# Banks for attention tiles ahead of the down groups, the first down groups in two parts at the turn of the halves, and one table load left out, in a kernel that mixes attention and a SwiGLU FFN

## Chip, cores, metric

The kernel runs on 1 core of one Trainium2 chip. The metric is the device time of one execution in microseconds (us); runs are given as median and range. The profile is that of one execution, with its own time.

## What is computed

`x` is 2048 x 576. The output mixes two branches by a gate per row:

```python
x = A_x
g = _sigmoid((x * gate_w).sum(-1, keepdims=True))
a = _A_ref(x, A_wq, A_wk, A_wv, A_wo, A_beta)   # 32 heads of 18, 4 segments of 512
b = _B_ref(x, B_w_gate, B_w_up, B_w_down)       # (silu(x @ w_gate) * (x @ w_up)) @ w_down
return g * a + (1 - g) * b
```

In `_A_ref` each segment has causal softmax attention within itself, `p @ v` of `softmax(q k^T)`, mixed by a gate per head with what a memory of the earlier segments returns; the heads' outputs, side by side, go through `wo`. The FFN's inner width is 4608.

## The kernel before

**Stages.** Up to about 220 us the kernel projects `q`, `k`, `v` and works the memory. Then one loop over `seq` (72 steps) does the FFN and, woven into it, the softmax attention. A last stage sends attention's output through `wo` and mixes. The FFN runs over two halves of 1024 rows; each half goes over 36 f-tiles of 128 of the inner width. fp32 operands are split into a high and a low part, and each product is made of three (`split`, L127: ScalarE copies the high part, L128; VectorE subtracts for the low part, L129; `split_by`, L939, does the same a beat apart, L940 and L941).

**One f-tile.** Seven products `seven(t, j)` (L993) build the gate and up projections of the tile from sums of blocks. Each is six matmuls of 512 columns at L998 and one at L1001. They accumulate in PSUM banks 0 (`a`), 1 (`x`) and 2 (`y`); ScalarE copies between them (L1058 among them) and VectorE adds. Two Silu (L1075, L1077) need their function's table on ScalarE, and `exp_table()` (L990) right behind them runs a dummy Exp of one column so that the Exp table is loaded again before attention's next Exp; so each f-tile shows two table loads, listed at L1075 and L991. The product of the two projections is `hh` (high) and `hl` (low). In the third tile of three its first half is split by L128 and L129 as one deferred step.

**The beats.** Between the products stand eight calls of `tick`, numbered 0 to 7, and each calls `beat(k, half)` (L943). A beat does, in this order: the steps deferred to it (`due`: loads, splits, weight sums), down groups in the number that `SHARE = (0, 0, 2, 2, 3, 3, 3, 3)` allows, and a step of the attention generator whenever its credit (`TICK`) reaches 1.

**Down groups.** After every third f-tile sixteen down groups are listed in `groups` (L1012), eight row blocks by two column parts of 320 and 256, each over the three f-tiles just made. A group is nine matmuls at L851, `hh`, `hh`, `hl` for each of three f-tiles; VectorE then copies it into `ya` (L854, the first time) or adds it (L856). They are worked in ticks 2 to 7 of the next f-tile, which is the first of the next three. At the turn of the halves, after f-tile 35 of the first half, there is no next tile in this half, and the sixteen groups are worked in ten beats of their own (`BREAK`, L1094), in which `x_second` (L966) also loads, sums and splits the second half's operands.

**Attention.** A step does several of: scores of a tile (`s_bank`, matmul L720 into a bank from `ts_tile`, row maxima by VectorE at L726), Exp of the previous tile (`e_bank`, ScalarE L738), high and low part of its result (VectorE L752, GpSimd L753), a transpose by DMA, and every sixth step the values (`v_unit`, matmuls L768 and L769 into one more bank from `ts_tile`, read by VectorE at L775).

**Banks.** Banks 0, 1 and 2 belong to `seven`. Group tiles take the one of banks 3, 4 and 7 that was taken longest ago. Score and value tiles take the one taken longest ago out of 5 and 6 while any group is listed, and out of 5, 6, 7, 3, 4 when none is. A matmul into a bank waits until the bank's former readers are done: the Exp (L738) of a score tile, L775 of a value tile, L854 or L856 of a group.

**The end.** When the attention generator has run out, `c_open` (L864) opens the last stage: it defers six loads of parts of `wo` and, by `c_load`, loads of attention's output `o` and the memory's part `me` of the first two row tiles. `c_tr` adds `me` to `o` on GpSimd (L913, L914) and transposes on TensorE (L917, L919); products with `wo` follow at L151. All DMAs are issued by the queue on SyncE (SP).

Of the kernel before, what the change touches and what calls it, by code (L numbers as in the profile page):

```python
# [12 lines left out]
F32 = mybir.dt.float32  # L13
# [7 lines left out]
P = 128  # L21
S = 2048
D = 576
# [4 lines left out]
FT = 36  # L28
# [7 lines left out]
CH = 3  # L36
# [5 lines left out]
HALF = ((2, 3), (0, 1))  # L42
TICK = ((0.57, 1.0), (0.47, 1.0))
QUIET = (5, 6, 7)
LEAD = 3
HIGH = (2, 3, 3, 7, 7, 8, 9)
LOW = (5, 6, 7, 8, 9, 10, 11)
# [18 lines left out]
def gated_mix(ctx, tc, xT, xrest, wf, wfr, wfh, wd, wv, wo, beta, cmask, ident, bmask, out):  # L66
    nc = tc.nc
# [18 lines left out]
    ps = pool(ctx, "ps", 1, space=bass.MemoryType.PSUM)  # L86
# [18 lines left out]
    pair_tile = banks(3, 4)  # L105
# [4 lines left out]
    x_tile = banks(1)  # L110
    y_tile = banks(2)
    taken = {}

    def oldest(*ids):
        n = min(ids, key=lambda i: taken.get(i, 0))
        taken[n] = len(taken) + max(taken.values(), default=0) + 1
        return n

    def ts_tile(shape=(P, L)):
        return ps.tile(list(shape), F32, name=f"bank{oldest(5, 6) if groups else oldest(5, 6, 7, 3, 4)}")  # L120

    def group_tile(shape=(P, L)):
        return ps.tile(list(shape), F32, name=f"bank{oldest(3, 4, 7)}")

    groups = []

# [153 lines left out]
    with ExitStack() as st:  # L280
# [310 lines left out]
        for s in range(NSEG):  # L591
# [41 lines left out]
            if s == 3:  # L633
# [50 lines left out]
    with ExitStack() as st:  # L684
# [3 lines left out]
        def defer(k, fn):  # L688
            while len(due) < k:
                due.append([])  # L690
            due[k - 1].append(fn)
# [146 lines left out]
            nc.sync.dma_start(f32(d).rearrange("p a n -> p (a n)"), dc[f])  # L838
            return d

        def down_group(c, i, hf, hs, ws, ya, half):
            b, k = divmod(i, 4)
            cs = (slice(0, 320), slice(320, D))[hf]
            t = (pair_tile if cps else group_tile)([P, 320])[:, :cs.stop - cs.start]
            n = 0
            for f in range(CH * c, CH * c + CH):
                hh, hl = (z[:, b, P * k:P * k + P] for z in hs[half, f])
                d = ws[half, f]
                dh, dl = d[:, 0], d[:, 1]
                for p, q in ((hh, dh), (hh, dl), (hl, dh)):  # L850
                    nc.tensor.matmul(t, p, q[:, cs], start=(n == 0), stop=(n == 3 * CH - 1))  # L851
                    n += 1
            if c == 0:
                nc.vector.tensor_copy(ya[:, i, cs], t)  # L854
            else:
                nc.vector.tensor_add(ya[:, i, cs], t, ya[:, i, cs])  # L856
            if c == FT // CH - 1 and hf and half == 0:
                stores.append((ffd[i], ya[:, i]))
# [5 lines left out]
        def c_open():  # L864
            if cps:
                return
            ast.close()
            cps.append(pool(st, "cp", 2, side="right"))
            for hf in range(2):
                wos.append(cps[0].tile([P, 2, NT, 288], F32R, name=f"wo{hf}", bufs=1))  # L870
            for n, (hf, z) in zip((1, 2, 4, 5, 8, 9), ((0, 0), (0, 1), (0, 2), (1, 0), (1, 1), (1, 2))):
                wo_load(n, hf, slice(96 * z, 96 * z + 96))
            defer(2, lambda: tiles.update({0: c_load(0)}))
            defer(3, lambda: nc.scalar.activation(gg, gg, AF.Exp, scale=-1.0))
            defer(4, gates)
            defer(6, lambda: tiles.update({1: c_load(1)}))

        def gates():
            nc.vector.tensor_scalar_add(gg, gg, 1.0)
# [63 lines left out]
        def beat(k=None, half=0):  # L943
            for fn in due.popleft() if due else ():
                fn()
            busy = 1 if groups else 0
            share = 2 if k is None else SHARE[k]
            for n in range(max(share, 1)):
                if groups and n < share:
                    down_group(*groups.pop(0))  # L950
                if n % 2 or (not busy and (n or k in QUIET)):
                    continue
                credit[0] += 0.5 if k is None else TICK[half][busy]
                if credit[0] >= 1:
                    credit[0] -= 1
                    if next(att, att) is att:
                        c_open()
# [32 lines left out]
        def exp_table():  # L990
            nc.scalar.activation(bg[:, 0:1], idt[:, 0:1], AF.Exp)  # L991
# [15 lines left out]
        for pos, (half, f) in enumerate(seq):  # L1007
# [67 lines left out]
            nc.scalar.activation(sg0, sg0, AF.Silu)  # L1075
# [120 lines left out]
```

## Time and profile before

| what | us |
|---|---|
| median of 3 runs | 1739.13 |
| range of the runs | 1737.43 to 1739.77 |
| the profiled execution, its own time | 1738.29 |
| its span in the trace | 1736.6 |
| TensorE busy | 1714.6 |
| VectorE busy | 1370.0 |
| ScalarE busy | 1094.1 |
| GpSimd busy | 935.1 |

The profiled execution lies 0.84 us under the median. Its time is 1.7 us longer than its span, which runs from the first to the last instruction. In a row of the timeline the first number is the start in us from the span's start, the second the length; then engine, line, operation, output and inputs with bank numbers left out, shape, and how many alike follow one another; in square brackets how long the engine was idle just before and what ended that. PE is TensorE, PEld its weight loads, DVE VectorE, ACT ScalarE, POOL GpSimd. Matmuls overlap: the next one starts before the last one's end, so ends lie later than the next start.

### The profile page before, as it was taken

How to read it: one execution, taken by the hardware profiler on the slowest of the kernel's cores; microseconds unless marked ns; L12 is line 12 of the kernel's file. 1: busy time of each engine (PE TensorE's matmuls, PEld its weight loads, DVE VectorE, ACT ScalarE, POOL GpSimd, SP SyncE). 2: the span in 40 equal slices, each digit the busy share in tenths (PEclk: the TensorE clock that was granted, in tenths of full speed). 3: DMA queues.
4: the chain of work that ended last, by engine and by line, in shares of the span. 5: the costliest groups of instructions: out<-in, count | busy, mean ns of one | idle time of the engine just before them, and what ended most of it. 6: DMA issues, size and time to landing. Idle time of an engine off the chain costs nothing.

```text
span 1736.6 us, 34910 instructions
## 1 busy us (share of the span) xinstructions
PE 1714.6 (99%) x11868; PEld 1482.5 (85%) x11868; DVE 1370.0 (79%) x3231; ACT 1094.1 (63%) x2198; POOL 935.1 (54%) x1194
## 2 busy tenths in 40 slices
PE   9999999999999999999999999999999999999999
PEld 7899978888888888887887788888888888888899
DVE  6557588988899889887989677787888777887655
ACT  7766585776677567666755755665766576566511
POOL 4434645666666656565666455555555555555121
PEclk9999999999999999999999999999999999999999
DMA  8654499999998889997879976776778677766544
GB/s 281 237 185 155 149 306 191 222 215 203 202 232 197 176 205 207 190 190 193 205 149 266 265 173 142 180 178 162 152 180 182 139 155 180 169 135 166 157 148 137
DMA packets 524002, 328.05 MB, mean 189 GB/s; under 512 B 411184, under 2 KB 460336, under 8 KB 523824
## 3 DMA queue, kind: packets, MB, share of 16 engines
q1 hardware_dynamic: 523824, 325.83, 76.6%
q8 instruction: 93, 1.52, 0.4%
q14 instruction: 85, 0.70, 0.1%
HBM read 165.76 MB, written 76.09 MB: 139 GB/s over the span
## 4 chain that ended last, share of the span: by engine, by line
PE 81%; ACT 9%; DVE 4%; DMA 2%; issue 2%; POOL 1%; SPq 1%; DVEq 0%; ACTq 0%; POOLq 0%
PE bank L998 30%; PE bank L851 26%; PE bank L151 10%; PE bank L1001 5%; PE bank L720 4%; PE bank L768 2%; ACT L1075 1%; PE bank L769 1%; ACT L991 1%; ACT pe L738 1%; PE bank L406 1%; PE bank L452 1%; ACT row L1075 1%; PE bank L342 1%; DVE hl L941 1%
## 5 line engine op out<-in xcount | busy, mean ns | idle before, releaser
L753 POOL TENSOR_TENSOR p<-pe,p 128x512 f16<-128x512 f32 x320 | 374.9, 1171 | 454.1 <-DVE p L752 437.4
L851 PE MATMUL bank<-dw,hh 128*128 128x320 f32 (+1 forms) x2304 | 489.9, 305 | 2.7 <-ACT hh L128 1.4
L851 PEld LDWEIGHTS bank<-dw,hh 128*128 128x128 f32 x2304 | 382.6, 190 | 14.0 <-DVE ya L856 1.6
L738 ACT ACTIVATE pe<-bank,mb 128x512 f32<-128x512 f32 (+3 forms) x512 | 246.4, 523 | 218.8 <-DVE mb L726 213.4
L851 PE MATMUL bank<-dw,hl 128*128 128x320 f32 (+1 forms) x1152 | 341.1, 296 | 0.2 <-DVE hl L129 0.2
L726 DVE CUSTOM_DVE_ANT_0 scr<-bank,cm 128x512 bf16<-128x512 f32 (+3 forms) x512 | 246.3, 481 | 7.9 <-PE bank L720 1.2
L851 PEld LDWEIGHTS bank<-dw,hl 128*128 128x128 f32 x1152 | 218.6, 190 | 0.4 <-DVE hl L129 0.4
L856 DVE TENSOR_TENSOR ya<-bank,ya 128x320 f32<-128x320 f32 x352 | 157.7, 453 | 72.3 <-PE bank L851 71.6
L1001 PE MATMUL bank<-xr,rh 128*128 128x512 f32 x504 | 196.5, 390 | 0.0
L746 POOL TENSOR_SCALAR_AFFINE_SELECT pe<-pe 128x256 f32<-128x256 f32 (+1 forms) x320 | 151.1, 473 | 31.3 <-ACT pe L738 20.2
L752 DVE CAST p<-pe 128x512 f16<-128x512 f32 x320 | 147.5, 461 | 0.0
L256 POOL TENSOR_TENSOR ws<-raw 128x256 f32<-128x256 f32 x140 | 123.6, 883 | 18.3 <-DMA raw<-in_wf_dram 7.2
L720 PE MATMUL bank<-kst,qst 108*128 108x512 bf16 (+3 forms) x512 | 125.4, 306 | 4.7 <-ACT pe L738 4.7
L1001 PEld LDWEIGHTS bank<-xr,rh 128*128 128x128 f32 x504 | 94.7, 188 | 20.5
L941 DVE TENSOR_TENSOR hl<-row,hh 128x512 fp32r<-128x512 f32 x120 | 101.6, 847 | 10.9 <-ACT hh L940 10.6
L1068 ACT ACTIVATE row<-bank 128x512 f32<-128x512 f32 x72 | 43.1, 599 | 94.6 <-PE bank L1001 94.5
L1075 ACT ACT_TABLE_LOAD x72 | 92.4, 1283 | 1.3
L1073 DVE TENSOR_TENSOR row<-bank,row 128x512 f32<-128x512 f32 x72 | 49.7, 690 | 55.0 <-ACT bank L1072 54.9
L991 ACT ACT_TABLE_LOAD x72 | 92.4, 1283 | 1.0
L151 PE MATMUL bank<-xo,qhi 128*128 128x512 f32 x264 | 83.1, 396 | 0.1
L1072 ACT ACTIVATE bank<-bank 128x512 f32<-128x512 f32 x72 | 42.0, 584 | 65.0 <-PE bank L1001 64.6
L256 POOL TENSOR_TENSOR ws<-raw,ws 128x256 f32<-128x256 f32 x70 | 56.6, 808 | 48.4 <-DVE wo__22573 L263 10.9
(2166 smaller groups left out, 4119.1 us busy)
## 6 DMA issues: line engine op xcount, KB each, us to landing
raw<-in_wf_dram SPq DMA_DIRECT2D x140, 256.0 KB
rh<-rc SPq DMA_DIRECT2D x72, 336.0 KB
dc<-dw SPq DMA_DIRECT2D x36, 576.0 KB
dw<-dc SPq DMA_DIRECT2D x36, 576.0 KB
stk<-q SPq DMA_DIRECT2D x32, 384.0 KB
draw<-in_wd_dram SPq DMA_DIRECT2D x36, 288.0 KB
rc<-rt SPq DMA_DIRECT2D x42, 224.0 KB
vd<-vps SPq DMA_DIRECT2D x8, 912.0 KB
```

The lines of the kernel that those rows point to most:

```text
L151: nc.tensor.matmul(t, st[n], mv[n], start=(n == 0), stop=(n == 13))
L256: (nc.gpsimd.tensor_sub if sub else nc.gpsimd.tensor_add)(src[j], p(), q())
L720: nc.tensor.matmul(t[:, c:c + w], qs[:KR, pr, P * i:P * i + P], ks[:KR, pr, 0:w], start=True, stop=True)
L726: nc.vector.tensor_tensor_reduce(scr[:, :w], t[:, c:c + w], cm[:, L - w:L], -SCALE, 3.0e38, OP.add, OP.min, m[:, k:k + 1])
L738: nc.scalar.activation(pe[:, c:c + w], t[:, c:c + w], AF.Exp, bias=m[:, k:k + 1], scale=SCALE)
L746: nc.gpsimd.affine_select(d, d, pattern=pat, compare_op=OP.is_ge, fill=0.0, base=0, channel_multiplier=1)
L752: nc.vector.tensor_copy(p[:, 0], pe)
L753: nc.gpsimd.tensor_sub(p[:, 1], pe, p[:, 0])
L851: nc.tensor.matmul(t, p, q[:, cs], start=(n == 0), stop=(n == 3 * CH - 1))
L856: nc.vector.tensor_add(ya[:, i, cs], t, ya[:, i, cs])
L998: nc.tensor.matmul(t, w[:, p, z], x[z][:, q], start=first and n == 0, stop=False, skip_group_check=True)
L1001: nc.tensor.matmul(t, rem[:, RPOS[j]], XR[j], start=False, stop=True, skip_group_check=True)
```

## The change

It has four parts. (1) `ts_tile` also gives bank 7 to score and value tiles while sixteen groups are listed, none popped yet, and the groups aren't the last of a half; banks 5, 6, 7, 3, 4 when none is listed, 5 and 6 else. What is "oldest" is told by a clock that goes on by one with each beat and each tile, on which a score or value tile counts as taken four later (`HELD`) and a group's tile one later. (2) At the turn the first three groups are popped after the first of the ten beats and computed by `down_parts`: for all three first the f-tiles 33 and 34, then f-tile 35. (3) `exp_table()` is left out in f-tile 35 of both halves. (4) `c_open` defers the first two `c_load` ahead of the loads of `wo`, the second at 3 beats in place of 6. The core of the diff:

```diff
+HELD = 4
...
+    clock = [0]
+
+    def soonest(ids, held):
         n = min(ids, key=lambda i: taken.get(i, 0))
-        taken[n] = len(taken) + max(taken.values(), default=0) + 1
+        clock[0] += 1
+        taken[n] = clock[0] + held
         return n
 
     def ts_tile(shape=(P, L)):
-        return ps.tile(list(shape), F32, name=f"bank{oldest(5, 6) if groups else oldest(5, 6, 7, 3, 4)}")
+        ids = (5, 6, 7, 3, 4) if not groups else (5, 6, 7) if groups[0][0] < FT // CH - 1 and len(groups) == 16 else (5, 6)
+        return ps.tile(list(shape), F32, name=f"bank{soonest(ids, HELD)}")
 
     def group_tile(shape=(P, L)):
-        return ps.tile(list(shape), F32, name=f"bank{oldest(3, 4, 7)}")
+        return ps.tile(list(shape), F32, name=f"bank{soonest((3, 4, 7), 1)}")
...
+        def down_group(*z):
+            down_parts([z], CH)
+
+        def down_parts(some, *cuts):
+            ts = []
+            for a, e in zip((0,) + cuts, cuts):
+                for m, (c, i, hf, hs, ws, ya, half) in enumerate(some):
...
+                    for f in range(CH * c + a, CH * c + e):
...
+                    if e == CH:
+                        down_end(ts[m], *some[m])
...
+            defer(2, lambda: tiles.update({0: c_load(0)}))
+            defer(3, lambda: tiles.update({1: c_load(1)}))
             for n, (hf, z) in zip((1, 2, 4, 5, 8, 9), ((0, 0), (0, 1), (0, 2), (1, 0), (1, 1), (1, 2))):
                 wo_load(n, hf, slice(96 * z, 96 * z + 96))
-            defer(2, lambda: tiles.update({0: c_load(0)}))
             defer(3, lambda: nc.scalar.activation(gg, gg, AF.Exp, scale=-1.0))
             defer(4, gates)
-            defer(6, lambda: tiles.update({1: c_load(1)}))
...
             busy = 1 if groups else 0
+            clock[0] += 1
...
-            exp_table()
+            if f < FT - 1:
+                exp_table()
...
                     for n in range(BREAK):
                         beat(None if n > 1 else n)
+                        if n == 0:
+                            down_parts([groups.pop(0) for _ in range(3)], CH - 1, CH)
```

Rows of the two programs follow at three places. The first is on TensorE in ticks 1 to 4 of an f-tile that is the first of three (L1001 is L1018 in the change, L720 L724, L998 L1015, L851 L862). Before:

```order
L1001 MATMUL bank2_8520<-xr1_1579,rh1_2332 128x512
L720 MATMUL bank5_8609<-kst1_2324,qst1_2323 128x512
L998 MATMUL bank0_8519<-xo20_2273,wo__8452 128x512 x3
...
L851 MATMUL bank3_8636<-dw_8240,hh_7662 128x320 x2
...
L720 MATMUL bank6_8656<-kst1_2324,qst1_2323 128x512
L851 MATMUL bank4_8662<-dw_8240,hh_7662 128x256 x2
...
L851 MATMUL bank7_8691<-dw_8240,hh_7662 128x320 x2
```

The same place in the change:

```order
L1018 MATMUL bank2_8520<-xr1_1579,rh1_2332 128x512
L724 MATMUL bank7_8609<-kst1_2324,qst1_2323 128x512
L1015 MATMUL bank0_8519<-xo20_2273,wo__8452 128x512 x3
...
L862 MATMUL bank3_8636<-dw_8240,hh_7662 128x320 x2
...
L724 MATMUL bank5_8656<-kst1_2324,qst1_2323 128x512
L862 MATMUL bank4_8662<-dw_8240,hh_7662 128x256 x2
...
L862 MATMUL bank3_8691<-dw_8240,hh_7662 128x320 x2
```

No row has moved; the first score tile is on bank 7 instead of 5, the next on 5 instead of 6, and the third group on bank 3, which the first group has just had, instead of 7.

The second place is TensorE at the turn, behind the last score tile of the first half (`bank6`) and around the value unit (L768 and L769, in the change L772 and L773); `dw_12713`, `dw_12852` and `dw_12969` are the down weights of f-tiles 33, 34 and 35. Before:

```order
L720 MATMUL bank6_13036<-kst1_2324,qst1_2323 128x256
L768 MATMUL bank5_13058<-v_11896,pt_12703 128x57
...
L769 MATMUL bank5_13058<-v_11896,pt_12945 128x38
L851 MATMUL bank3_13115<-dw_12713,hh_12131 128x320 x2
...
L851 MATMUL bank3_13115<-dw_12852,hh_12669 128x320 x2
L851 MATMUL bank3_13115<-dw_12852,hl_12670 128x320
L851 MATMUL bank3_13115<-dw_12969,hh_12861 128x320 x2
```

In the change:

```order
L724 MATMUL bank6_13035<-kst1_2324,qst1_2323 128x256
L862 MATMUL bank7_13044<-dw_12713,hh_12131 128x320 x2
...
L862 MATMUL bank3_13051<-dw_12713,hh_12131 128x256 x2
...
L862 MATMUL bank4_13058<-dw_12713,hh_12131 128x320 x2
...
L862 MATMUL bank4_13058<-dw_12852,hl_12670 128x320
L862 MATMUL bank7_13044<-dw_12969,hh_12861 128x320 x2
L862 MATMUL bank7_13044<-dw_12969,hl_12862 128x320
L862 MATMUL bank3_13051<-dw_12969,hh_12861 128x256 x2
...
L772 MATMUL bank5_13090<-v_11896,pt_12703 128x57
```

Three groups have moved ahead of the value unit, their products with f-tiles 33 and 34 first and those with f-tile 35, which need the newest `hh` and `hl`, last; the value unit's bank 5 is now one whose former score tile is read by the Exp at the turn (third place).

The third place is ScalarE at the turn; `row_12867` holds the Silu of the gate, `hh_12861` is the last tile's high part, and `pe` is attention's Exp. Before:

```order
L1075 ACT_TABLE_LOAD
L1075 ACTIVATE row_12867<-row_12867 128x512
L1077 ACTIVATE row_12868<-bank2_12920 128x512
L991 ACT_TABLE_LOAD
L991 ACTIVATE bg_82<-idt_79 128x1
L128 ACTIVATE hh_12861<-row_12867 128x512
L738 ACTIVATE pe_13032<-bank7_12987,mb1_2326 128x128
```

In the change:

```order
L1092 ACT_TABLE_LOAD
L1092 ACTIVATE row_12867<-row_12867 128x512
L1094 ACTIVATE row_12868<-bank2_12920 128x512
L132 ACTIVATE hh_12861<-row_12867 128x512
L742 ACT_TABLE_LOAD
L742 ACTIVATE pe_13031<-bank5_12987,mb1_2326 128x128
```

The load of the Exp table has moved behind the copy of `hh`, to the first Exp that needs it, and the dummy Exp is gone. In the last f-tile of the second half, where no Exp of attention follows, ScalarE has three rows less.

More of the change, by code (lines that the diff above doesn't have):

```diff
@@ L112, in gated_mix @@
     taken = {}
-    def oldest(*ids):
+    clock = [0]
+    def soonest(ids, held):
         n = min(ids, key=lambda i: taken.get(i, 0))
-        taken[n] = len(taken) + max(taken.values(), default=0) + 1
+        clock[0] += 1
+        taken[n] = clock[0] + held
         return n
     def ts_tile(shape=(P, L)):
-        return ps.tile(list(shape), F32, name=f"bank{oldest(5, 6) if groups else oldest(5, 6, 7, 3, 4)}")
+        ids = (5, 6, 7, 3, 4) if not groups else (5, 6, 7) if groups[0][0] < FT // CH - 1 and len(groups) == 16 else (5, 6)
+        return ps.tile(list(shape), F32, name=f"bank{soonest(ids, HELD)}")
     def group_tile(shape=(P, L)):
-        return ps.tile(list(shape), F32, name=f"bank{oldest(3, 4, 7)}")
+        return ps.tile(list(shape), F32, name=f"bank{soonest((3, 4, 7), 1)}")
     groups = []
@@ L839, in d_fetch, with down_end @@
             return d
-        def down_group(c, i, hf, hs, ws, ya, half):
-            b, k = divmod(i, 4)
-            cs = (slice(0, 320), slice(320, D))[hf]
[L844 to L852, printed above, removed]
+        def down_group(*z):
[4 more added lines that the diff above has]
+                for m, (c, i, hf, hs, ws, ya, half) in enumerate(some):
+                    b, k = divmod(i, 4)
+                    cs = (slice(0, 320), slice(320, D))[hf]
+                    if a == 0:
+                        ts.append((pair_tile if cps else group_tile)([P, 320])[:, :cs.stop - cs.start])
+                    n = 3 * a
+                    for f in range(CH * c + a, CH * c + e):
+                        hh, hl = (z[:, b, P * k:P * k + P] for z in hs[half, f])
+                        d = ws[half, f]
+                        dh, dl = d[:, 0], d[:, 1]
+                        for p, q in ((hh, dh), (hh, dl), (hl, dh)):
+                            nc.tensor.matmul(ts[m], p, q[:, cs], start=(n == 0), stop=(n == 3 * CH - 1))
+                            n += 1
+                    if e == CH:
+                        down_end(ts[m], *some[m])
+        def down_end(t, c, i, hf, hs, ws, ya, half):
+            cs = (slice(0, 320), slice(320, D))[hf]
             if c == 0:
```

## Prediction

> **What bounds the kernel now.** The first view is the profile page, its totals of busy time and its chain of work that ended last:
>
> ```profile
> span 1736.6 us, 34910 instructions
> PE 1714.6 (99%) x11868; PEld 1482.5 (85%) x11868; DVE 1370.0 (79%) x3231; ACT 1094.1 (63%) x2198; POOL 935.1 (54%) x1194
> ...
> PE 81%; ACT 9%; DVE 4%; DMA 2%; issue 2%; POOL 1%; SPq 1%; DVEq 0%; ACTq 0%; POOLq 0%
> ```
>
> TensorE (PE) sets the time, and its matmuls stay the same in number and shape. So the change can win only where PE stands still or runs at a low clock, 22 us of idle time and a little more. The second view, PE's waits (total, times, longest, in us), says where; its two largest rows:
>
> ```profile
> PE bank L720 <- ACT pe L738: 4.7, 6, 1.2
> PE bank L768 <- ACT pe L738: 3.1, 2, 1.9
> ```
>
> Eight waits, 7.8 us, are attention tiles (scores at L720, values at L768) whose PSUM bank still holds scores that the Exp at L738 has not read. Three more, at the turn and at the end of the loop, come below. The third view is the timeline around one of the eight, ACT first and then PE:
>
> ```profile
> 619.74 1.28 ACT L1075 ACT_TABLE_LOAD   x1
> ...
> 622.17 1.28 ACT L991 ACT_TABLE_LOAD   x1
> ...
> 625.52 0.81 ACT L738 ACTIVATE pe<-bank,mb 128x256 f32<-128x256 f32 x2
> ```
>
> ```profile
> 624.85 0.39 PE L1001 MATMUL bank<-xr,rh 128*128 128x512 f32 x1
> ...
> 626.39 0.38 PE L720 MATMUL bank<-kst,qst 108*128 108x512 bf16 x1 [1.16 <-ACT pe L738]
> ```
>
> ACT comes out of two table loads late, reads bank 5 until 626.33, and PE starts 0.06 us later. A printed wait is shorter than the stop. To see it, the pace of matmuls is wanted:
>
> ```profile
> 954.02 1.55 PE L998 MATMUL bank<-xo,wo__13048 128*128 128x512 f32 x6
> ```
>
> Six end 1.55 us after the first starts and one lasts 0.39, so starts are (1.55 - 0.39) / 5 = 0.23 us apart. From 624.85 the next start was due at 625.08 and came at 626.39: a stop of 1.31 where 1.16 is printed. With 0.15 to 0.17 added each, the eight stops are 7.8 + 8 x 0.16 = **9.1 us**.
>
> The longest is a value unit, and the windows of granted clock (PE, PEld, DVE, ACT, POOL busy, then clock, DMA share, GB/s) show what follows it:
>
> ```profile
> 808.15 0.19 PE L768 MATMUL bank<-v,pt 128*128 128x57 bf16 x1 [1.88 <-ACT pe L738]
> ```
>
> ```profile
> 805.59:809.00 3.41, 1.53 (x36) 1.15 (x36) 1.98 (x6) 3.41 (x10) 0.48 (x1) 1.00 0.87 225
> 809.00:812.41 3.41, 3.41 (x21) 2.77 (x18) 2.05 (x5) 1.45 (x4) 3.41 (x5) 0.50 0.47 84
> ```
>
> PE was busy for 1.53 of 3.41 us and then ran at clock 0.50 for the next 3.41 us, which costs 1.7 us of work.
>
> **Banks, the gain.** All eight stops stand at tick 1 of a first tile of three, when sixteen down groups are listed and none is popped. There the rows shown with the change put the tile on bank 7. In the tile above, its reader would be the last 512-column Exp ahead, and the product behind the stop needs the copy L1058:
>
> ```profile
> 612.15 0.67 ACT L738 ACTIVATE pe<-bank,mb 128x512 f32<-128x512 f32 x1
> ```
>
> ```profile
> 624.19 0.58 ACT L1058 ACTIVATE bank<-bank 128x512 f32<-128x512 f32 x1
> ```
>
> Bank 7 is free from 612.82, 12 us ahead (7 in the closest of the eight), and the copy is done at 624.77, ahead of 625.3, when PE now comes. So I take all: -9.1 for the stops, -1.7 for the half clock, and -0.3 for small waits of this kind: **-11.1 us**. Bounds: nothing below this, since no other stop of this kind exists; above it half, -5.5, if each stop is only passed on to the next reader of ACT.
>
> The Trainium skill speaks against the 1.7: "TensorE: Matmul & The Clock Gate", Part 1, What's actually happening, has the clock halve after an idle window of about 3.4 us. By it a stop of 2.05 us would not have halved anything, and the gain here would be 9.4 instead of 11.1. The half clock that I charge at the turn below, and rival (2), would fall away as well. The two windows disagree: one 45% busy was enough, so I keep the 1.7.
>
> **Banks, the price.** Bank 7 was the bank of the third down group (320 columns). Now that group takes bank 3, the first group's, and waits until DVE has added the first group to `ya`:
>
> ```profile
> 631.82 0.48 DVE L856 TENSOR_TENSOR ya<-bank,ya 128x320 f32<-128x320 f32 x1
> ```
>
> ```profile
> 632.49 0.45 PE L851 MATMUL bank<-dw,hh 128*128 128x320 f32 x2
> ```
>
> PE would arrive 1.31 earlier, at 631.18; the add ends at 632.30 and hands over 0.05 later; the wait is 1.17 us. DVE does not come earlier with PE, for its queue there runs through splits that follow ACT's table loads. A tile that had no stop pays too:
>
> ```profile
> 390.28 0.48 DVE L856 TENSOR_TENSOR ya<-bank,ya 128x320 f32<-128x320 f32 x1
> ```
>
> ```profile
> 390.00 0.45 PE L851 MATMUL bank<-dw,hh 128*128 128x320 f32 x2
> ```
>
> The add ends at 390.76, so the group at 390.00 would wait 0.81. The last of the eight stops, 1.39 long, gives:
>
> ```profile
> 1596.90 0.48 DVE L856 TENSOR_TENSOR ya<-bank,ya 128x320 f32<-128x320 f32 x1
> ```
>
> ```profile
> 1598.54 0.45 PE L851 MATMUL bank<-dw,hh 128*128 128x320 f32 x2
> ```
>
> 1597.43 less (1598.54 - 1.39) is 0.28. The same subtraction in the other 19 tiles gives five more waits between 0.21 and 0.40, 1.5 together, margins of 0.15 to 0.99 in six and over 1.3 in eight. Sum 1.17 + 0.81 + 0.28 + 1.5 = **+3.8 us**. Bounds: +1.5 if DVE comes 0.3 earlier, +7.5 if it comes 0.4 later throughout (8 x 0.4 more, and two margins used up).
>
> **The turn.** PE, then DVE and ACT, then the windows:
>
> ```profile
> 927.32 0.39 PE L720 MATMUL bank<-kst,qst 108*128 108x256 bf16 x2
> ...
> 931.07 0.56 PE L851 MATMUL bank<-dw,hh 128*128 128x320 f32 x2 [1.35 <-ACT hh L128]
> 931.80 0.59 PE L851 MATMUL bank<-dw,hl 128*128 128x320 f32 x1 [0.17 <-DVE hl L129]
> ...
> 937.71 0.50 PE L851 MATMUL bank<-dw,hh 128*128 128x256 f32 x2 [1.34 <-DVE ya L856]
> ```
>
> ```profile
> 928.53 0.69 DVE L1082 TENSOR_TENSOR row<-bank,row 128x512 f32<-128x512 f32 x1 [0.19 <-ACT row L1075]
> ...
> 931.05 0.69 DVE L129 TENSOR_TENSOR hl<-row,hh 128x512 fp32r<-128x512 f32 x1 [1.23 <-ACT hh L128]
> ```
>
> ```profile
> 929.00 1.28 ACT L991 ACT_TABLE_LOAD   x1
> 930.30 0.20 ACT L991 ACTIVATE bg<-idt 128x1 f32<-128x1 f32 x1
> 930.41 0.61 ACT L128 ACTIVATE hh<-row 128x512 fp32r<-128x512 f32 x1
> 930.93 0.82 ACT L738 ACTIVATE pe<-bank,mb 128x128 f32<-128x128 f32 x2
> ```
>
> ```profile
> 928.46:931.88 3.42, 1.90 (x21) 1.38 (x16) 2.12 (x4) 3.39 (x8) 0.14 (x1) 1.00 1.03 327
> 931.88:935.29 3.41, 3.41 (x15) 3.41 (x16) 3.15 (x8) 2.69 (x6) 3.13 (x4) 0.50 1.04 384
> 935.29:938.70 3.41, 2.06 (x15) 1.67 (x14) 3.41 (x6) 0.09 (x1) 3.41 (x3) 1.00 1.09 312
> ```
>
> Before, the stops are 1.5, 0.3 and 1.5, and the half clock costs 1.7: 5.0 us. In the change `hh` of the last tile is copied from about 929.3, when its product (L1082) is there, to 929.9, and the load follows. PE does 18 matmuls of the two older tiles from 927.5; by the pace per column (0.23 x 320/512 = 0.14, for 256 0.12) that is six rounds of 0.14 + 0.12 + 0.14, 2.4 us, up to 929.9, so `hh` costs no wait. `hl` follows 0.7 us behind, at 930.6, and stops PE 0.4; the value unit, whose bank the Exp frees at 929.9 + 1.28 + 0.82 = 932.0, stops it another 0.4. No window falls under 2 us of work. PE is 5.0 - 0.8 = 4.2 us ahead.
>
> That lead meets others. The second half's products need operands that DVE splits, in a stretch where DVE has no slack, and then weights that come by DMA:
>
> ```profile
> 931.00:955.10 24.10, 22.51 (x149) 21.28 (x150) 23.71 (x49) 9.35 (x19) 17.41 (x15) 0.93 1.12 302
> ```
>
> ```profile
> 950.00:967.00 17.00, 16.90 (x124) 13.94 (x122) 10.52 (x25) 8.62 (x17) 7.15 (x8) 1.00 1.05 302
> ```
>
> ```profile
> 967.19 1.17 PE L998 MATMUL bank<-xo,wo__13458 128*128 128x512 f32 x4 [0.29 <-DMA wo__13458<-wc]
> ```
>
> DVE is busy 23.7 of 24.1 us and starts its part only 1.1 us earlier (`hh` at 929.9 instead of 931.0), so some 3 us of the lead are left behind it. The 16 DMA engines are full (1.12 and 1.05) up to the block wo__13458, for which PE waits already; it cannot land much earlier, I take 0.7 us. PE so waits 2.3 us or more longer there, under half a window of work may result, and then the clock halves as above, 1.7 us. Bounds: -3.0 if the block moves with the rest, +1.7 if nothing moves and the clock halves; I take -0.7 + 1.7 = **+1.0 us**, as DMA is full in every row.
>
> The removed load here only changes places with `hh`; ACT makes no difference beyond this.
>
> **The end.** There the load goes altogether, and `o` and `me` of the second tile go ahead of two weight loads:
>
> ```profile
> 1645.78 0.66 PE L917 MATMUL bank<-idt,o 128*128 128x128 f32 x4 [1.09 <-POOL o L913]
> ```
>
> ```profile
> 1644.26 1.47 POOL L913 TENSOR_TENSOR o<-o,me 128x576 f32<-128x576 f32 x1 [8.24 <-DMA me<-med]
> ```
>
> The add that PE waits for was released by the load of `me`; landing some places earlier it is done before PE comes, and PE saves 1.09 + 0.16 = 1.2 us. The two weight loads are later by that much and are needed later. Bounds 0 and -1.5; I take **-1.2 us**.
>
> ACT also drops 1.28 + 0.20 us here, which no wait of PE asks for. "ScalarE: Activation LUTs", What ACT_TABLE_LOAD costs, of the Trainium skill puts a switch at 2.66 us with a drain behind the load. In the rows above the next ACTIVATE starts 0.02 us after the load's end, at 930.30, so there is no such drain here; by the page `hh` at the turn would come 2.7 us earlier, not 1.1, and the forecast would be the same, since DMA sets the end there.
>
> **Sum**: -11.1 + 3.8 + 1.0 - 1.2 = -7.5 us. The profiled execution took 1738.29 us, so 1730.8; the median of the runs is 1739.13, 0.84 above it: **1731.6 us**.
>
> **Rivals.** (1) *The turn pays*: the block comes with PE; the turn gives -3.0 instead of +1.0: 1727.6. For it: PE's wait for the block is only 0.29 now, so its place in the queue may hang on what PE itself releases. Against it: shares over 1. (2) *More half clocks*: a third group's wait falls with other stops into one window with under 2 us of work, twice, +1.7 each: 1735.0. For it: 1.90 of 3.42 was enough, 2.06 was not. Against it: the largest new wait, 1.17, leaves 2.2. (3) *Slower*: the third groups wait everywhere. The price hangs on DVE's adds alone: every one of the 22 tiles has that wait or a margin before it. If the Exp of the tile that got bank 7 now comes up to 1.3 us earlier ahead of `hh`, and the splits and so the adds come 1.3 later, eight waits grow by that and six margins are used up: 3.8 + 10.4 + 4.6 = 18.8, 15 more than forecast: 1746.6. Break-even is at about 0.75 us. Against it: the order of ACT and DVE changes only at the turn and the end, and ACT works without a pause through the stop at 626. (4) *The change does little*: the stops only pass to the next score tile, -5.5 instead of -11.1: 1737. Against it: the banks are free 7 us ahead.
>
> **Chances**: forecast 0.57, (1) 0.17, (2) 0.10, (4) 0.08, (3) 0.08. The forecast's own terms spread it over 1729 to 1734. Range 1726 to 1737.5, which takes in (1), (2) and (4). 0.2% or 3.5 us is about what can be told from no change here: faster takes the forecast, (1) and half of (2) and more, 0.80; within 0.2% 0.12; slower 0.08.
>
> **What would show it.** No wait of L720 or L768 (new lines L724, L772) for Exp of more than 0.3 us at a tick 1; the window after 809 at clock 1.00; waits of a third group (L862) for DVE's add (L872) in eight tiles, 1.2 the longest; the first wait at the turn gone, and a longer one for a weight block after it; at the end no wait for POOL's add. It is wrong if the adds come later than 0.7 us, if new half clocks appear in the first tiles of three, or if the blocks after the turn are there when PE comes.

## The result, and the profile after

The changed kernel takes 1734.35 us in the median of 12 runs (1731.88 to 1736.27), the kernel before 1738.45 in 12 runs taken beside it (1735.97 to 1739.77). The ratio is 0.9978, interval 0.997 to 0.9985: 3.8 us faster, with an interval of 2.6 to 5.2. The forecast was 7.5 us faster. The profiled execution after took 1734.02 us, 4.27 less than the one before. Its page:

```profile
span 1732.2 us, 34907 instructions
...
PE 1713.1 (99%) x11868; PEld 1479.3 (85%) x11868; DVE 1373.7 (79%) x3231; ACT 1092.4 (63%) x2195; POOL 936.7 (54%) x1194
```

PE has lost 1.5 us of busy time and 3 us of idle time. Where the idle time stands has changed more than its sum does. PE's waits in the loop and the last stage after, those that have no counterpart before, or a smaller one (total, times, longest):

```profile
PE bank L1015 <- DMA wo__13415<-wc: 3.0, 1, 3.0
PE bank L862 <- DVE ya L872: 2.1, 3, 0.9
...
PE bank L1015 <- ACT bank L1089: 1.0, 2, 0.8
PE bank L1015 <- DVE xo L133: 0.9, 1, 0.9
PE bank L772 <- DMA pt<-p: 0.9, 1, 0.9
```

All eight waits for the Exp (4.7 and 3.1 us before) are gone from the list. In their place stand one for a weight block behind the turn, three for VectorE's adds into `ya` (and five that are too short for this list), one at the end, one for VectorE's split of the second half's operand `xo`, and one for a transposed operand.

**A first tile of three.** PE around the score tile that stopped for 1.31 us before, and VectorE's add:

```profile
625.37 0.39 PE L1018 MATMUL bank<-xr,rh 128*128 128x512 f32 x1
625.60 0.39 PE L724 MATMUL bank<-kst,qst 108*128 108x512 bf16 x1
...
632.75 0.56 PE L862 MATMUL bank<-dw,hh 128*128 128x320 f32 x2 [0.91 <-DVE ya L872]
```

```profile
632.22 0.48 DVE L872 TENSOR_TENSOR ya<-bank,ya 128x320 f32<-128x320 f32 x1
```

The score tile follows in 0.23 us, without a stop. Seven microseconds later the third group waits for an add that ends at 632.70, 632.30 before; this trace runs 0.5 us later here, so the add has kept its place. From start to start the stop is 1.07 us. The group's first two matmuls then take 0.56 us together, 0.45 before: the second starts 0.25 us behind the first and not 0.15, so the group loses another 0.1.

**The half clock that was there, and a new one.** The stretch around the value unit that waited 1.88 us, and the one around the new wait for a weight block:

```profile
805.59:809.00 3.41, 3.41 (x52) 2.78 (x51) 1.62 (x5) 3.40 (x10) 0.00 (x0) 1.00 1.00 251
809.00:812.41 3.41, 3.41 (x24) 3.16 (x23) 3.38 (x9) 1.98 (x6) 3.35 (x4) 1.00 0.33 67
960.04:963.45 3.41, 0.46 (x3) 0.33 (x3) 0.00 (x0) 3.11 (x5) 0.00 (x0) 1.00 0.97 212
963.45:966.86 3.41, 3.41 (x10) 2.62 (x9) 0.62 (x2) 0.00 (x0) 0.00 (x0) 0.50 1.18 315
```

The first pair now runs full at clock 1.00. In the second PE worked 0.46 us of a window and had half the clock in the next.

**The turn**, ACT and then PE's two stops in the moved part:

```profile
927.20 0.63 ACT L132 ACTIVATE hh<-row 128x512 fp32r<-128x512 f32 x1 [0.28 <-DVE row L1100]
927.85 1.28 ACT L742 ACT_TABLE_LOAD   x1
929.14 0.84 ACT L742 ACTIVATE pe<-bank,mb 128x128 f32<-128x128 f32 x2
```

```profile
928.61 0.42 PE L862 MATMUL bank<-dw,hl 128*128 128x320 f32 x1 [0.16 <-DVE hl L133]
930.03 0.19 PE L772 MATMUL bank<-v,pt 128*128 128x57 bf16 x1 [0.21 <-DMA wo__13005<-in_xT_dram]
```

`hh` comes ahead of the load, and PE stops 0.33 us for `hl` and 0.36 for the value unit (start to start). The second row names a DMA. That load has nothing to do with the value unit; its bank's Exp ended at 929.14 + 0.84 = 929.98, and PE went on 0.05 us later; in the trace of held0, below, the row at this place names that Exp. Then the second half begins:

```profile
947.69 1.68 PE L1015 MATMUL bank<-xo,wo__13080 128*128 128x512 f32 x6
...
951.17 0.48 PE L1015 MATMUL bank<-xo,wo__13172 128*128 128x512 f32 x1
952.57 1.42 PE L1015 MATMUL bank<-xo,wo__13172 128*128 128x512 f32 x5 [0.92 <-DVE xo L133]
...
959.77 0.39 PE L1018 MATMUL bank<-xr,rh 128*128 128x512 f32 x1
963.11 2.60 PE L1015 MATMUL bank<-xo,wo__13415 128*128 128x512 f32 x6 [2.95 <-DMA wo__13415<-wc]
965.50 0.63 PE L1018 MATMUL bank<-xr,rh 128*128 128x512 f32 x1
965.93 1.98 PE L1015 MATMUL bank<-xo,wo__13457 128*128 128x512 f32 x6
```

The first product starts at 947.69 against 954.02 before, 6.3 us ahead; the next f-tile's first product at 965.93 against 967.19, 1.3 ahead. Five of the 6.3 us have gone. The third product stops inside for VectorE's split of `xo`: a start was due at 951.17 + 0.23 = 951.40 and came at 952.57, 1.2 us. The wait for the weight block took 3.1 (a start was due at 960.00), and the half clock 1.2 up to 965.93 and 0.4 behind it; the kernel before stands 0.45 at its own block, which comes off. What SP issued just before explains which transfers were in front:

```profile
952.24 5.49 SPq L1056 DMA_DIRECT2D ffd<-ya  x8
957.82 0.88 SPq L709 DMA_DIRECT2D wo__13415<-wc  x1
```

Eight stores of the first half's result, 8 x 288 KB = 2.36 MB, went into the queue between 952.2 and 957.7, and the block that PE waited for behind them.

**The end.** PE's new stop and ACT's queue ahead of it:

```profile
1639.98 1.65 PE L1015 MATMUL bank<-xo,wo__22997 128*128 128x512 f32 x6 [0.78 <-ACT bank L1089]
```

```profile
1636.16 0.61 ACT L907 ACTIVATE wo<-raw 128x480 fp32r<-128x480 f32 x1 [1.60 <-DMA raw<-in_wo_dram]
...
1638.18 0.60 ACT L907 ACTIVATE wo<-raw 128x480 fp32r<-128x480 f32 x1 [0.92 <-DMA raw<-in_wo_dram]
...
1639.32 0.60 ACT L1089 ACTIVATE bank<-bank 128x512 f32<-128x512 f32 x1
```

The wait for GpSimd's add is gone. But two copies of `wo` stand in ACT's queue waiting for their loads, and the copy L1089, which PE needs, stands behind them.

**A gain table.** For a sum over stages I compare the start of each f-tile's first product in the two traces; a row says how much a kernel's lead over the kernel before grew in the stretch (us, one profiled execution each, own working from the traces).

| kernel | f-tiles 2 to 35 | turn and f-tiles 36 to 39 | f-tiles 40 to 71 | from there to the end |
|---|---|---|---|---|
| the change | 2.1 | -1.6 | 3.4 | 0.5 |
| banks_only | 1.9 | -0.1 | 3.3 | -0.1 |
| turn_only | -0.5 | -1.6 | 0.0 | -0.6 |
| old_late | -0.5 | -1.3 | 0.0 | -0.6 |
| end_only | 2.2 | -0.9 | -0.4 | 0.6 |
| late_stores | 1.6 | 1.8 | 3.4 | 0.5 |
| held0 | 2.3 | -1.8 | 4.9 | 0.2 |
| held0_late | 2.7 | 0.6 | 4.7 | 0.6 |
| held0_spread | 3.8 | 0.6 | 4.6 | -0.2 |
| best_old_turn | 3.5 | 0.1 | 4.5 | 0.3 |
| best_keep_load | 2.4 | -0.1 | 4.7 | 0.5 |
| late_copies | 2.0 | 2.5 | 4.7 | 0.1 |
| spread_held4 | 3.2 | 1.5 | 3.0 | 0.3 |

The third column repeats within 0.4 us for the same rule of banks. The first does not: end_only, whose code is that of before up to the turn, has 2.2 there, and turn_only and old_late, with the same code there, have -0.5. So a difference under 3 us in the first stretch of one trace says nothing about banks. Before f-tile 2 the traces differ by another 2 us at most.

### The profile page after: what moved, and what is told of

It reads as the page before. It is cut to its first block, busy times and chain, and to the rows that moved or that the text cites. A ratio compares the mean times of both kernels' runs of the same rounds, so it can differ in the third digit from the quotient of the medians.

```text
span 1732.2 us, 34907 instructions
## 1 busy us (share of the span) xinstructions
PE 1713.1 (99%) x11868; PEld 1479.3 (85%) x11868; DVE 1373.7 (79%) x3231; ACT 1092.4 (63%) x2195; POOL 936.7 (54%) x1194
## 4 chain that ended last, share of the span: by engine, by line
PE 80%; ACT 6%; DVE 6%; DMA 3%; issue 2%; POOL 1%; SPq 1%; DVEq 0%; ACTq 0%; POOLq 0%
PE bank L1015 31%; PE bank L862 25%; PE bank L155 10%; PE bank L1018 5%; PE bank L724 4%; PE bank L772 2%; PE bank L773 1%; ACT L1092 1%; PE bank L410 1%; DVE scr L730 1%; DVE hl L957 1%; DVE p L756 1%; PE bank L456 1%; ACT L1008 1%; DVE xo L133 1%
## 5 line engine op out<-in xcount | busy, mean ns | idle before, releaser
L862 PE MATMUL bank<-dw,hh 128*128 128x320 f32 (+1 forms) x2304 | 489.7, 305 | 2.6 <-DVE ya L872 2.1
L862 PEld LDWEIGHTS bank<-dw,hh 128*128 128x128 f32 x2304 | 380.5, 190 | 16.7 <-DVE ya L872 5.7
L862 PE MATMUL bank<-dw,hl 128*128 128x320 f32 (+1 forms) x1152 | 340.3, 295 | 0.2 <-DVE hl L133 0.2
L862 PEld LDWEIGHTS bank<-dw,hl 128*128 128x128 f32 x1152 | 217.9, 189 | 0.4 <-DVE hl L133 0.4
L1018 PE MATMUL bank<-xr,rh 128*128 128x512 f32 x504 | 196.5, 390 | 0.0
L724 PE MATMUL bank<-kst,qst 108*128 108x512 bf16 (+3 forms) x512 | 125.5, 306 | 0.0
L1018 PEld LDWEIGHTS bank<-xr,rh 128*128 128x128 f32 x504 | 94.7, 188 | 20.5
L1089 ACT ACTIVATE bank<-bank 128x512 f32<-128x512 f32 x72 | 42.0, 584 | 67.2 <-PE bank L1018 66.8
L1075 ACT ACTIVATE bank<-bank 128x512 f32<-128x512 f32 x72 | 41.6, 578 | 66.2 <-PE bank L1018 66.2
```

The lines of the kernel that those rows point to most:

```text
L724: nc.tensor.matmul(t[:, c:c + w], qs[:KR, pr, P * i:P * i + P], ks[:KR, pr, 0:w], start=True, stop=True)
L862: nc.tensor.matmul(ts[m], p, q[:, cs], start=(n == 0), stop=(n == 3 * CH - 1))
L1018: nc.tensor.matmul(t, rem[:, RPOS[j]], XR[j], start=False, stop=True, skip_group_check=True)
```

## Experiments

Each ratio is to runs of the kernel before taken beside it.

**banks_only**: the change without its turn and its end.

```diff
-            if f < FT - 1:
-                exp_table()
+            exp_table()
...
-                        if n == 0:
-                            down_parts([groups.pop(0) for _ in range(3)], CH - 1, CH)
```

The two loads by `c_load` are back in their old places as well.

> Only the change of banks (bank 7 in ticks 0 and 1, the clock, HELD); the turn and the end as before. Theory A, read from the trace after: the eight stops and the half clock after the value unit go, the third groups' waits cost 3 to 4 us, a value unit of the first such tile waits 0.8 us longer for its transposed operand: 5.0 us faster than before, ratio 0.9971. Theory B, the forecast's terms: 7.3 us faster, ratio 0.9958. Theory C, the stops only pass on: 2 us or less, ratio 0.9988 or more.

Measured: 1734.06 us, ratio 0.9973 (0.9963 to 0.9983), 4.7 us faster. Theory A's 0.9971 lies within the interval, theory B's 0.9958 and theory C's 0.9988 outside. The banks alone give what the whole change gives. Two things in its trace are not as theory A had them. The value unit of the first such tile does not wait for its transposed operand at all. And at the turn the new rule for banks makes a stop of its own where the old turn is kept, with a half clock behind it (929.22 to 932.64):

```profile
928.84 0.19 PE L772 MATMUL bank<-v,pt 128*128 128x57 bf16 x1 [4.10 <-ACT pe L742]
```

The waits of the kernel before at this place, 1.35 and 1.34 us, are gone, and the sum is the same (-0.1 in the table).

**turn_only**: the old rule for banks and the old end, with the new turn.

```diff
-        ids = (5, 6, 7, 3, 4) if not groups else (5, 6, 7) if groups[0][0] < FT // CH - 1 and len(groups) == 16 else (5, 6)
-        return ps.tile(list(shape), F32, name=f"bank{soonest(ids, HELD)}")
+        return ps.tile(list(shape), F32, name=f"bank{oldest(5, 6) if groups else oldest(5, 6, 7, 3, 4)}")
...
-            if f < FT - 1:
+            if f < FT - 1 or half:
```

> Only the turn (three groups in two parts, no early load of the Exp table there); banks and end as before. Theory A: PE comes some 4 us earlier to the second half and loses them to a wait of about 3 us for a weight block that comes by DMA, and to a half clock window behind it: 1.2 us slower than before, ratio 1.0007. Theory B, the turn pays: 3 us faster, ratio 0.9983.

Measured: 1741.15 us, ratio 1.0012 (1.0003 to 1.0021): slower, as theory A said, by 2.1 us by the ratio (its 1.2 lies within the interval), but not for its reason: no wait for a weight block stands in this trace. It shows a cost that neither theory had. PE's stop in the new groups, and the two windows behind it:

```profile
933.39 0.90 PE L860 MATMUL bank<-dw,hh 128*128 128x320 f32 x2 [2.80 <-ACT pe L740]
```

```profile
929.31:932.72 3.41, 1.28 (x10) 1.07 (x9) 3.14 (x8) 3.11 (x5) 1.04 (x2) 1.00 0.95 303
932.72:936.13 3.41, 2.74 (x10) 2.74 (x11) 0.34 (x2) 3.41 (x8) 2.37 (x3) 0.50 1.03 376
936.13:939.54 3.41, 3.41 (x49) 3.21 (x48) 2.00 (x5) 0.01 (x1) 1.00 (x1) 0.50 1.10 274
```

By the old rule one of the three groups takes bank 7, whose score tile is the one that the Exp at the turn reads, and this Exp now stands behind the table load. So the turn without the new rule for banks costs time; the parts do not add.

**end_only**: `c_load` ahead and no table load in the last f-tile; the rest as before.

```diff
-                        if n == 0:
-                            down_parts([groups.pop(0) for _ in range(3)], CH - 1, CH)
...
-            if f < FT - 1:
+            if f < FT - 1 or not half:
```

The rule for banks is the old one, as in turn_only.

> Only the end (o and me of the first two row tiles loaded earlier, no load of the Exp table in the last f-tile); banks and turn as before. Theory A: the wait of 1.1 us for GpSimd's add goes, and 0.9 us of it come back as a wait for ScalarE's copy in the last f-tile, whose queue stands behind copies of wo: 0.3 to 0.5 us faster, ratio 0.9998. Theory B, the forecast: 1.2 us faster, ratio 0.9993.

Measured: 1739.80 us, ratio 1.0004 (0.9996 to 1.0013). No gain can be told; the forecast's 0.9993 lies outside the interval, theory A's 0.9998 inside. The gain table has 0.6 us for it. This trace also shows something of the half clock. Before the turn it has the code of the kernel before, and the same wait of the value unit:

```profile
807.57 0.19 PE L770 MATMUL bank<-v,pt 128*128 128x57 bf16 x1 [1.88 <-ACT pe L740]
```

```profile
803.09:806.50 3.41, 2.60 (x13) 1.72 (x12) 1.96 (x4) 3.38 (x8) 0.65 (x1) 1.00 0.98 287
806.50:809.92 3.42, 2.35 (x46) 2.13 (x46) 3.06 (x9) 3.36 (x9) 1.98 (x3) 1.00 0.36 104
809.92:813.33 3.41, 3.41 (x24) 3.16 (x23) 3.31 (x7) 0.00 (x0) 3.41 (x5) 1.00 0.79 176
```

Here the stop falls across two windows, 2.60 and 2.35 us of work, and no half clock follows. So the 1.7 us that I credited to the change at 809 are there only when the stop falls into one window: in the traces of before, turn_only and old_late, not in this one.

**late_stores**: the change, with the eight stores two f-tiles later.

```diff
-                if k == 0:
+                if k == 0 and f == 2:
                     while stores:
...
-            if f == 0:
+            if f == CH:
                 yas[half] = yp.tile([P, 8, D], F32, name="ya")
```

> The whole change, and the eight stores of the first half's result (ffd, 2.3 MB) issued two f-tiles later, at the start of the third f-tile of the second half instead of the first. Theory A, the DMA engines are what takes the turn's gain: the wait of 3.1 us for the weight block and the half clock behind it go or shrink to under 1 us, 3 to 4.5 us faster than the change: 1730, ratio to before 0.995. Rival, the block waits for its buffer or for the queue's other loads: no difference to the change, 1734, ratio 0.998. A cost of it: copies into ya in the fourth f-tile may wait for the stores.

Measured: 1731.41 us, ratio 0.9959 (0.9946 to 0.9971), 2.9 us under the change. The stretch behind the turn, late_stores and then the change:

```profile
955.00:967.00 12.00, 12.00 (x89) 9.57 (x88) 7.64 (x16) 8.07 (x14) 4.87 (x6) 1.00 1.07 283
```

```profile
955.00:967.00 12.00, 9.05 (x68) 7.04 (x67) 4.21 (x11) 5.94 (x10) 2.90 (x4) 0.86 1.04 305
```

PE works through all of the 12 us, with DMA as full as in the change, 1.07 and 1.04. SP's queue shows why, in late_stores and then in the change:

```profile
954.14 0.70 SPq L808 DMA_DIRECT2D kst<-stk  x2
954.95 0.34 SPq L709 DMA_DIRECT2D wo__13406<-wc  x1
```

```profile
951.49 0.70 SPq L808 DMA_DIRECT2D kst<-stk  x2
```

wo__13406 is here the block for which the change waited. It is issued 0.8 us behind the loads of `kst`, where the change issues it 6.3 us behind them, at 957.82, with the stores in between. What took most of the turn's gain is the place of the stores in the queue. Theory A stands, if it is read as the queue and not as the DMA engines being full. The 1.2 us at VectorE's split of `xo` stay, here and in every kernel with the new turn; no kernel with the old turn has this wait. The cost was another than expected: no copy into `ya` makes PE wait, but the weights `rh` of the fourth f-tile do, whose load stands behind the stores (six of the eight in the first row):

```profile
976.21 3.35 SPq L1056 DMA_DIRECT2D ffd<-ya  x6
...
984.48 0.36 SPq L250 DMA_DIRECT2D rh<-rc  x1
```

```profile
989.43 0.50 PE L1018 MATMUL bank<-xr,rh 128*128 128x512 f32 x1 [1.52 <-DMA rh<-rc]
```

**old_late**: the kernel before with that edit alone.

> The kernel before, with the eight stores of the first half's result two f-tiles later (as in late_stores) and nothing of the change. If the late stores pay only because the change brings PE to the second half's weight blocks ahead of them (theory A), they give nothing here: 0 to 0.5 us faster for the 0.3 us wait at the block, up to 1.8 us slower where copies into ya wait for the stores; ratio 1.0000 to 1.0010. If they pay by themselves (rival: less DMA traffic at the turn helps any version), 2 to 3 us faster, ratio 0.9985.

Measured: 1740.20 us, ratio 1.0008 (0.9999 to 1.0016): no gain, rather a loss, by the wait for `rh` (1.56 us at 994.46 in its trace). Late stores pay only with the new turn; the rival falls.

**held0**: the change with one number changed.

```diff
-HELD = 4
+HELD = 0
```

A score tile then does not count as taken later than it was, and the third group takes bank 7 back in place of the first group's bank.

> The whole change with HELD 0 instead of 4: by the rows of order the third group of a first f-tile then takes bank 7, whose score tile is read well ahead, instead of the bank that the first group has just left. Theory A, the price of the banks is this choice alone: the waits of third groups for DVE's add go, 3.5 to 3.9 us faster than the change: 1730.6, ratio to before 0.9956. Rival, the waits move to the Exp of the score tile on bank 7: no difference to the change, ratio 0.9977.

Measured: 1733.59 us, ratio 0.9969 (0.9958 to 0.9981), 0.8 us under the change by the medians and 1.6 by the ratios; the interval does not part it from the change. All waits of third groups for VectorE are gone, and waits for the Exp are back, later in the same f-tiles, behind two table loads as in the first place. PE and then ACT in held0:

```profile
642.12 0.19 PE L772 MATMUL bank<-v,pt 128*128 128x57 bf16 x1 [0.64 <-ACT pe L742]
...
646.78 0.38 PE L724 MATMUL bank<-kst,qst 108*128 108x512 bf16 x1 [0.98 <-ACT pe L742]
```

```profile
642.08 1.28 ACT L1092 ACT_TABLE_LOAD   x1
...
644.50 1.28 ACT L1008 ACT_TABLE_LOAD   x1
...
645.90 0.82 ACT L742 ACTIVATE pe<-bank,mb 128x256 f32<-128x256 f32 x2
```

In the second half, where the table's third column is steady, it is 1.5 us better (4.9 against 3.4); in the first, 2.8 us of third groups' waits (start to start) went, and four waits for Exp of 0.8 to 1.1 us stand where two of 0.2 did. Neither theory holds for the whole: the price is the choice of bank in one half, and is passed on in the other.

**held0_late** and **held0_spread**: both terms together. In held0_spread the stores go one per tick of the second f-tile:

```diff
-                if k == 0:
-                    while stores:
+                if f == 1:
+                    if stores:
                         nc.sync.dma_start(*stores.pop(0))
```

> The change with HELD 0 and with the stores two f-tiles later: the two terms are in different places and should add: 2.9 us (measured) and 3.7 us (expected) faster than the change, 1727.7, ratio to before 0.9938. If the third groups' waits are only a symptom of ScalarE's lateness, it stays at 1731, ratio 0.9959.

> As held0_late, but the eight stores are issued one per tick in the second f-tile of the second half, so that they have landed before the copies into ya of the fourth: in late_stores these copies stop PE for about 1.8 us there. Theory A: that 1.4 to 1.8 us goes too, 1726, ratio to before 0.9929. Rival: one f-tile earlier they hold up that tile's weight blocks again, part of the 3.1 us wait comes back: 1728 to 1730.

Measured: 1730.98 us, ratio 0.9953 (0.9941 to 0.9964), and 1729.46 us, ratio 0.9941 (0.9929 to 0.9953). The two terms add, to a little less than expected; held0_spread is the fastest of all, 9.5 us under the kernel before by the medians, with an interval below that of the change (0.997 at its lower end). The wait that theory A put down to copies into `ya` was the one for `rh`, and it is gone, but the f-tiles from there on lose 0.6 us twice, and another wait of 1.5 us stands at the second f-tile's first product, which spread_held4 with the same stores does not have. Between the two kernels the intervals overlap.

**best_old_turn** and **best_keep_load**: held0_spread with the old turn, and with the new turn but the early table load kept.

```diff
-            if f < FT - 1:
+            if f < FT - 1 or not half:
                 exp_table()
```

This edit stands in both; best_old_turn has the call of `down_parts` out as well.

> held0_spread with the turn of the kernel before (no group in two parts, early load of the Exp table kept there). Theory A: once the stores stand no longer ahead of the weight blocks the new turn pays; without it PE comes to the second half some 4 us later, of which 2 to 2.5 us remain at the fourth f-tile: 2.5 us slower than held0_spread, 1732, ratio to before 0.9957. Rival, the turn is worth nothing either way: same as held0_spread, 0.9941.

> held0_spread with the early load of the Exp table kept at the turn (three groups in two parts kept). Theory A: hh of the last f-tile is copied 1.1 us later again (930.4 instead of 929.3 in the time of before), PE waits 1.0 to 1.2 us for it behind the 18 early matmuls, and the value unit's wait of 0.4 us goes: 0.7 us slower than held0_spread at the turn, of which little is left at the weight blocks, ratio 0.9941 to 0.9946. Rival, the load was the turn's main cost: 2 us slower.

Measured: 1730.71 us, ratio 0.9952 (0.994 to 0.9964), and 1729.78 us, ratio 0.9948 (0.9936 to 0.9961). The medians have the order of theory A and half its sizes (1.25 and 0.3 us over held0_spread; 1.9 and 1.2 by the ratios); the intervals overlap that of held0_spread, so the times settle nothing here. In the traces the second column has 0.1 for the old turn, -0.1 for the new one with the load kept, and 0.6, 0.6, 1.5, 1.8 and 2.5 for the five with the new turn and late stores (-1.6 and -1.8 with the stores in front). So once the stores are out of its way the three groups together with the later table load are worth 0.5 to 2.4 us in single traces, and 1.8 to 3.7 of the lead of 4.3 still go at the next f-tiles. The old turn of best_old_turn is not that of the kernel before: it has the stop of 4.1 us of banks_only.

**late_copies**: held0_spread with two of ScalarE's copies of `wo` three beats later.

```diff
-            defer(n + 5, lambda: nc.scalar.activation(wos[hf][:, 0, :, c], box[0], AF.Copy))
+            m = n + 3 if n in (4, 5) else n
+            defer(m + 5, lambda: nc.scalar.activation(wos[hf][:, 0, :, c], box[0], AF.Copy))
```

VectorE's subtraction moves with it.

> held0_spread with the third and fourth copy of wo on ScalarE (L907) three beats later. Theory A: in the last f-tile these copies stand in ScalarE's queue waiting 1.9 and 1.3 us for their loads and hold up the copy L1089, for which PE stands 1.6 us; PE's stop goes, 1.0 to 1.6 us faster than held0_spread, ratio 0.9934. Rival, the products with wo then wait for the later copies: no gain, 0.9941.

Measured: 1730.52 us, ratio 0.9948 (0.9936 to 0.996), no gain. The wait for L1089 is gone, and this row is new:

```profile
1639.49 0.54 PE L155 MATMUL bank<-wo,oh 128*128 128x288 f32 x2 [1.01 <-DVE wo L909]
```

The rival holds: the copies did hold up L1089, and PE now waits for their results instead. At the end the loads of `wo` are what comes last.

**spread_held4**: held0_spread with HELD 4 again.

> The change as it is (HELD 4) with the eight stores one per tick in the second f-tile of the second half; beside held0_spread it gives the worth of HELD 0 once more. Theory A: half of what the waits of third groups cost (2 of 3.8 us) came back in held0 as waits for Exp in the first half: 1.0 to 1.5 us slower than held0_spread, 1730.7, ratio 0.9949. Rival, no worth: 0.9941.

Measured: 1730.84 us, ratio 0.9953 (0.9942 to 0.9965), 1.4 us over held0_spread, theory A's size, though the intervals overlap. It comes from the second half, though, not the first: 3.0 against 4.6 in the third column.

## Why the prediction was right or wrong

The direction held and the time lay in the range. The gain was half of the 7.5 us, so the terms one by one.

*Banks, the gain* (-11.1). All eight stops went, 9.1 us. The half clock at 809 went in this pair of traces, but end_only shows that the kernel before does not have it in each execution, so the term held something that is not the kernel's own, and its coming true here is partly luck. Another stop went the other way, 29 us behind the first of the eight:

```profile
291.92 0.20 PE L772 MATMUL bank<-v,pt 128*128 128x57 bf16 x1 [0.92 <-DMA pt<-p]
```

Start to start this stop is 1.07 us, 0.24 before: of the 1.08 us gained at 262, 0.83 went here. That is not the change's doing either: with the same rule for banks it is 0 in banks_only and 0.04 in spread_held4, and with the old rule 0.71 in turn_only. What decides it stays open. Two small waits for Exp, 0.19 each, came as well (707 and 828), and one of 0.21 went (447), of the 0.3 that the term has for such.

*Banks, the price* (+3.8). Eight third groups waited, those eight that I had found, for 0.24, 0.81, 1.07, 0.69, 0.30, 0.30, 0.21 and 0.26: 3.9 us. That VectorE's adds keep their time when PE comes earlier was right. The term still was too small: in each of the eight the second matmul started 0.1 us later too, 0.8 together, so the price was 4.7. By the times, banks_only has 4.7 us of gain where the two terms have 7.3.

*The turn* (+1.0). The table has -1.6, of which 0.4 is the price of a third group at f-tile 39: +1.2. The steps came as worked out: no stop for `hh`, 0.33 for `hl` (0.4), 0.36 for the value unit (0.4), a lead of 4.3 us from the turn up to the second half's first product (4.2), 1.2 of it lost at VectorE's splits (1.1), then a wait of 3.1 us for a weight block and the half clock. The block was wo__13415, an earlier one than the one I named. The reason was half right. I gave the full DMA engines; late_stores shows them as full with PE not waiting for a load there. It is the order in the queue, with stores ahead that nothing needed soon.

*The end* (-1.2). This step failed in its size: 0.5 in the trace, nothing in end_only's time. "The two weight loads are later by that much and are needed later" was wrong, for ScalarE's copies of them stand in its queue in front of the copy that PE needs. The stop of 1.2 us went, and one of 0.9 came.

*The sum.* The two profiled executions differ by 4.3 us, 3.2 less than forecast: 0.9 for the third groups, 0.8 for the transposed operand, 0.7 at the end, 0.4 for the two small Exp waits, 0.2 at the turn; 0.2 is left over.

Of the rivals, more half clocks (2) was nearest in its time, 1735.0 against 1734.35, but by luck: the trace after has no half clock in a first tile of three, only the one behind the turn that the forecast itself has. That the stops only pass on (4), 1737, held for few of them; held0 shows it at work on a larger scale in the first half. That the turn pays (1) fell for the change, and late_stores shows that the stores stood in its way. The slower one fell: VectorE's adds were not late.

## What to carry to other kernels

When a wait is taken away ahead of a busy queue, follow the engine's lead forward to each thing that runs by its own clock (a table load, an add chain, an operand's split, a load), and count the lead as gained only up to the first that is late; here 6.3 us shrank to 1.3 within one f-tile. A full DMA queue is not by itself a bound: ask which of the transfers ahead is not needed yet, and move that one. And a change that reorders work should be tried with the old resources too, for the two may only work together.

## What the runs showed of the hardware

The traces narrow down when the clock halves. In the 14 traces, cut into windows of 3.41 us by the places where the clock changed, all nine windows of the FFN loop in which PE was busy for 1.63 us or less were followed by one at 0.50. Of five with 1.86 to 1.90 us two were, those with 1.89 and 1.90; one of 1.78 near the end of turn_only was not. Of some 80 with 1.97 to 2.8 us none was, but for one that itself ran at 0.50 (turn_only, 932.72, with 2.74). So the border lies between 1.63 and 1.97 us, 48% to 58% of a window, and within it PE's busy time, whose ends are modelled, does not tell. A stop of 2 us costs 1.7 us more or nothing, by where it falls.
